# Memory attention with a spatial gate on one core: the memories' products in two single PSUM banks instead of one tile of two banks

## The chip, the cores and the metric

The kernel runs on one core of one Trainium2 chip. What is measured is the time of the whole program on the device in microseconds, lower is better: a median of runs, and beside it one execution that the hardware profiler took, from which all rows below come.

## The reference, cut to what matters

Eight batches b, eight heads of width 64, 576 positions, 32 memories a head. An attention over memories is followed by a feed-forward layer with a spatial gate:

```
a = softmax(phi);  k_m = a^T k;  v_m = a^T v          # 32 memories a head
attn = softmax(scale * q k_m^T) v_m                   # 576 x 64 a head
x = attn, heads side by side                          # 576 x 512 a batch
h = relu(x @ w_in); u, v = halves of h                # 512 columns each
v_n = (v - mean(v)) / sqrt(var(v) + 1e-6)             # over the 512 columns
v_s = w_spatial @ v_n + b_spatial                     # over the 576 positions
out = (u * v_s) @ w_out
```

## The kernel before, in words

The attention's output is never formed. `products` multiplies the memories' values `vT` by `w_in` first; the result, "the memories' products" mp, is 256 memories (two halves r of 128 partitions) by 1024 columns (two halves f of 512: f = 0 for u, f = 1 for v). The attention weights then multiply it. Every full-precision product is made of three products of short parts: a value x is kept as a high part (mh, ah, vh, gh) and a low part (ml, al, vl, gl), and the terms high x high, high x low and low x high are summed in PSUM.

The work is cut into steps, each written as a Python generator that yields after every piece. The capital letter is the kind, the digit the tile:

- P: weights of the memories from phi (DMA, maxima on DVE, transposes mt and mb on PE, `cmb` on ACT, subtraction on DVE, exponential on ACT, sums `es` on POOL or DVE).
- K: `kvm` (144 small matmuls), the sums' reciprocal `den`, `kmn` and `vmn` on ACT, the transposes `tk` and `tv`, copies `kT` and `vT`.
- Q: q by DMA, four transposes `qT` on DVE. S: scores `sc` on PE into four banks (r, c), four transposes out of them on DVE (L547), the softmax on DVE and ACT (`rmx`, `sm`, `rsum`), transposes `aT`, then `ah` on ACT and `al` on DVE for either half.
- M0, M1: the products for f = 0 and 1: the matmuls mp (L603) for both halves r in turn, then, half by half, `mh` on ACT (L612) and `ml` on DVE (L153; for a few of the first two batches by PE and ACT). 
- V0 to V4: rows of v: `pv` on PE, relu on ACT, mean and variance on DVE (`bn`, L681), a few numbers on POOL (`few`), normalisation on ACT, `vh` on ACT and `vl` on DVE.
- U0 to U3: `pu` on PE in two halves, relu `u` on ACT. G0 to G3: the spatial product `ps` on PE in four pieces (the first three take `vh`, `vl` of V0, V1, V2; the last V3 and V4), then `g` on DVE (L769), `gh` on ACT, `gl` on DVE. O0 to O4: `po` on PE in two halves, copy `o` on ACT, DMA out.

Below, ps1.0 is the first piece of G1, pu0.1 the second half of U0, po3.0 the first half of O3.

Nothing reorders the steps. Three tables of letters, `START` (first batch, with the loading and decoding of the weights), `PLAN` (the body of the loop, batches 1 to 5) and `END` (the last two batches) say in which order the pieces are written, a mark ' meaning the next batch. Every engine works its own instructions in the written order, and SP's DMA queue too, so a waiting instruction holds up all that stands behind it on its engine. Z in `START` is a matmul on a constant whose result nobody reads (`warm_up`, tile `idle`); there are 25 of them.

PSUM has eight banks. Two pools share them: four tiles of one bank (`bank`) and two tiles of two banks (`banks`):

```
    ps1 = ctx.enter_context(tc.tile_pool(name="ps1", bufs=4, space=PSUM))
    ps2 = ctx.enter_context(tc.tile_pool(name="ps2", bufs=2, space=PSUM))
```

A new tile waits until the last reader of the tile that had its place is done. Before, mp, pu and ps share the two tiles of two banks; sc, kvm, pv, po and the small transposes share the four single banks.

Of the kernel before, what the change touches and what calls it, by code (L numbers as in the profile page):

```python
# [19 lines left out]
START = """  # L20
    P Z P*2 Z P*2 Q P*9 Q P Q P Q K Q*4 K Q*2 P Z Q Z Q Z D1 K W E0 K W K*2 Z D0 K*2 E0*2 Z K*4
    S Z S K S*2 W S T1 D1 Z L0 S*2 T1 D0 Z X0 T4 Z T3 Z T3 S T1 S X1 T1 S E1 Z E0 S*3 Z T4 Z T4
    T3 L0 Z S*2 L1 T3 E1 S Z T4 Z*2 T0 S E1 S T4 X1 Z E1 T0 S L0 L1 T0 S*2 Z M1*2 S*2 X1 L0 L1
    P' S M1 L1 P' X0 P' T2 Z X0*2 M1 B S M1 B Q' K' S P' M1 S T2 P' M0 S V0 M0*2 V0 T2 P' Z V4
    M0 P'*3 V2 V1 V0 Z T2 M0 V4 X1 U1 P' X0 P' V0*2 X0 V0 M0 V1 V0 P' V3 P' M0 U1 V2 V4 V1 X0 K'
    P' V4 U0 P' V2 U1 U0 K' Q' K' V4 U0 V1*2 V2 V1 U2*2 V2 Q' V1 U3 Z U3 U2 V3 V4 G1 V2 V3 U3
    P'' G1 Q' K' V4 V3 X1 V2 V4 G1 G2*2 Q' V3 G2 K' V3 V4*2 P'' V3 K'*2 P'' G2 X1 Q' K' P'' G2
    X1 X3 P'' K'' G2 K' X2 G2 K'' K' G1 P'' X3 P'' X3 P'' G1 X3 G0 G1 G0 G1 K' G1*2 G0 P''*2 G0
    X2 G3 G2 K' P'' G3 X2 G2 S' M1' X2 G0 X2 P'' G3 G0*2 S'*2 O0 P'' X2 X3 G3 X2 X3 S' O2 X3 S'
    M1'*2 S' G3 G0 O3 G3 G0 G3 S' M1' O3 O1 S'*2 O3 P'' O1 P'' S' Q'' O1 S' G3 M1' S' G3 O0 S'  # L30
    O3 O2 S' M1' S' O0 S'*5 O2 K'' O0 K'' Q'' O2 O1 K''*2
"""

PLAN = """
    M0 V0 V4 V1 V0 U1 U3 V2 V0 U3 U0 K' U0 V1*2 Q' P'' V2 V3 P'' V4 V0 V1 P'' U2*2 V3 S' V2*2 U0
    M0' M1' V3 S' S S' P'' U2 P''*2 V2 K'' M0'*2 V3 M0'*2 M1'*2 K'' G1 M1' V3 G1 V2 V4 P'' M1'
    P'' K''' S' G0*2 V3 V2 V4*2 G1 V3 P''' G0 S' G0 S' G1 G3 K'' S' G0 G3 S' G3 G0 G2*2 G1 K''*3
    M1' K'' G1 S' G0 G1 P''' G0 S'*2 G1 G3 O1 S' G2 G1 S' M0 S' P''' G3 S'*2 G3 G0 G3 G2 O0 G3*2
    S'*2 G2 Q'' O2 G2 S' V1' G2 O1 V0' O3 V1' O1 V1' P''' O1 G2 O0 O1 V0' M1 O0 G2 K'' U3' Q''
    S' O3 V0' V4' O2 P''' Q'' O4 K'' Q'' O3 V4' O0 O4 V4' U1'*2 P''' O2 V4' O4 O2 O4 O0 V4' P'''  # L40
    K'' Q'' K''' O3
"""

END = """
    V0 V1 V4 V1 V0 V1 K' U3*2 V0 V2 V0 U2 V2 U1 U2 V1 V3 V2*2 U2 V2 V3 U0*2 M0' U0 M1' Q' S' V4
    M0' V3 G1 M0'*2 M1' G1 V3 M0' M1'*2 V3 G0 M1' V2 V4 S' V2 V3 G0 G1 V4 S' G0 S'*2 V3 V4 S' G0
    S' G0 S' G1 G3 G0 G1 G0 S' G3 G1 G3 S' G3 S'*2 U1 G2 S' G2 G0 G1 G0 V4 G2*2 S'*3 G1 O3 S' G1
    G3 U1' S'*2 V0' V2' S' V1' G2 V0' U1' V1' U1' V0' O0 U0' O2 U0' U3' V2' G2 V3' U0' G3 V4 G2
    V1' V2' V0'*2 G3 O2 G2 V0' U2' V2' U2' V0' O0 V2' U3' U2' G3*2 V1' G0' V4' V1' V3' O3 V2'
    V1' V3' V1' V4' O0 G0' V3' V4' U3' G1' V3' V4' V2' V3' V4' O1 Q' G0' G2 G1' V3' V4'*2 O1 V4'  # L50
    Q' G1' O3 V4'*2 G1'*3 G0' G2' G1' G2'*2 G1' G0' G2' G0' G3' G0'*2 O1 G3' G0' G3'*2 O2 O0 O1'
    G3' O1 G3' G1' G2'*2 O4' O3' G2' O2 O0' G2' G3' O1'*3 O0' O3' G3' V4 O3' O3 O3' G2' G3' K'
    O0' O4' O0' O2' O4' O2'*2 O4' O2'
"""
# [837 lines left out]
```

## Time and profile before

| what | value |
|---|---|
| median of 3 runs | 436.64 us (435.97 to 437.99) |
| the profiled execution | 436.06 us, of which the span of instructions is 434.3 us |
| PE (TensorE matmuls) busy | 405.9 us, 93% of the span |
| DVE / ACT / POOL busy | 275.1 / 230.6 / 102.5 us |
| PE in the first 50 us | 38.3 us busy |
| mean granted TensorE clock | 0.979 of full |
| bytes moved | 50.68 MB, mean 117 GB/s |

PE is the engine that is nearly always at work, so what another engine does matters where PE stands still for it. The profile draws a matmul longer than the step to the next one (a pair of 288 columns is drawn 0.42 us long and the next pair begins after 0.26 us), so idle time that it prints for PE is a little less than what was lost.

### The profile page before, as it was taken

To read this page: it belongs to the slowest core of one execution; us is meant where nothing else is said; L and a number is where in the kernel's file an instruction comes from. 1 tells how busy PE (TensorE), PEld (TensorE's weight loads), DVE (VectorE), ACT (ScalarE), POOL (GpSimd) and SP (SyncE) were. 2 spreads that over 40 slices of the span, in tenths; PEclk is the share of its full clock that TensorE was granted. 3 is DMA by queue.
4 is the path that set the end of the run, shared out by engine and by line. 5 is a ranking of instruction groups with operands and counts; after the bars stand their busy time and mean duration, and the time that the engine had idled before them with its cause. 6 is when DMAs were issued, how large, how long until landed. Compare 5 with 4: busy or idle time off the path is not lost.

```text
span 434.3 us, 9318 instructions
## 1 busy us (share of the span) xinstructions
PE 405.9 (93%) x3882; PEld 344.1 (79%) x3882; DVE 275.1 (63%) x492; ACT 230.6 (53%) x444; POOL 102.5 (24%) x191
## 2 busy tenths in 40 slices
PE   3799999998989999999899999999899998999996
PEld 2675689786789887988698887988698877888985
DVE  3269548886889257974589357964697347934420
ACT  2538797446754377345753376335853374337412
POOL 1376473203200114012501014022401110023100
...
GB/s 305 365 381 249 74 76 207 146 27 250 150 208 12 105 163 129 110 26 154 83 219 2 103 183 160 60 54 142 121 2 2 127 51 2 0 2 24 2 48 145
DMA packets 85725, 50.68 MB, mean 117 GB/s; under 512 B 66162, under 2 KB 70258, under 8 KB 85684
## 3 DMA queue, kind: packets, MB, share of 16 engines
...
q14 instruction: 11, 0.09, 0.1%
...
## 4 chain that ended last, share of the span: by engine, by line
PE 47%; DVE 20%; ACT 14%; DMA 8%; POOL 5%; issue 4%; SPq 1%; POOLq 0%; DVEq 0%; ACTq 0%
PE po L798 18%; PE ps L758 14%; PE pv L636 6%; PE pu L720 4%; ACT vr L693 4%; DMA raw<-in_moe_w_in_dram 3%; DVE ml L153 3%; DVE vl L698 3%; DVE rmx L553 2%; DVE sm L556 2%; ACT mh L612 2%; DMA out_dram<-o 2%; ACT vh L696 2%; DVE phi_sb L311 2%; DMA q_sb<-in_q_dram 1%
## 5 line engine op out<-in xcount | busy, mean ns | idle before, releaser
L758 PE MATMUL ps<-wth,vh 128*128 128x288 f32 x256 | 57.3, 305 | 7.4 <-DVE ml L153 4.1
L758 PE MATMUL ps<-wtl,vh 128*128 128x288 f32 x256 | 54.6, 294 | 0.0
L758 PE MATMUL ps<-wth,vl 128*128 128x288 f32 x256 | 54.5, 294 | 0.0
L758 PEld LDWEIGHTS ps<-wth,vh 128*128 128x128 f32 x256 | 40.8, 188 | 13.1 <-issue 4.4
L798 PE MATMUL po<-woh,gh 128*128 128x512 f32 x128 | 50.4, 394 | 0.2 <-DVE sm L547 0.2
L798 PE MATMUL po<-wol,gh 128*128 128x512 f32 x128 | 50.3, 393 | 0.0
L798 PE MATMUL po<-woh,gl 128*128 128x512 f32 x128 | 50.2, 392 | 0.0
L804 ACT COPY o<-po 128x512 f32<-128x512 f32 x36 | 21.1, 585 | 46.1 <-PE po L798 35.1
L758 PEld LDWEIGHTS ps<-wtl,vh 128*128 128x128 f32 x256 | 41.4, 188 | 0.0
L758 PEld LDWEIGHTS ps<-wth,vl 128*128 128x128 f32 x256 | 40.9, 188 | 0.0
L681 DVE BATCH_NORM_STATS2 st<-vr 128x6 f32<-128x512 f32 (+1 forms) x35 | 24.0, 684 | 22.9 <-ACT vr L678 22.8
L684 POOL TENSOR_SCALAR few<-few 128x1 f32<-128x1 f32 (+1 forms) x35 | 9.7, 276 | 120.1 <-DVE few L682 105.3
L693 ACT ACTIVATE vr<-vr,few 128x512 f32<-128x512 f32 (+1 forms) x40 | 32.5, 815 | 8.9 <-POOL few L688 8.9
L586 POOL CAST ar<-ah 128x128 fp32r<-128x128 f32 x7 | 6.1, 874 | 130.2 <-ACT ah L579 130.2
L433 DVE STREAM_TRANSPOSE qT<-q_sb 128x576 f32<-128x576 f32 x28 | 20.2, 753 | 23.6 <-DMA q_sb<-in_q_dram 19.0
L698 DVE TENSOR_TENSOR vl<-vr,vh 128x512 fp32r<-128x512 f32 x32 | 22.0, 691 | 20.5 <-ACT vh L696 19.6
L720 PE MATMUL pu<-ah,mh 128*128 128x288 f32 x128 | 28.9, 307 | 0.1
L579 ACT CAST ah<-aT 128x576 fp32r<-128x576 f32 x14 | 9.4, 675 | 36.3 <-DVE aT L575 36.3
L798 PEld LDWEIGHTS po<-woh,gl 128*128 128x128 f32 x128 | 24.1, 188 | 5.5
L153 DVE TENSOR_TENSOR ml<-mp,mh 128x512 fp32r<-128x512 f32 x28 | 18.8, 688 | 15.1 <-ACT mh L612 15.1
L798 PEld LDWEIGHTS po<-woh,gh 128*128 128x128 f32 x128 | 24.1, 188 | 5.1 <-issue 0.4
L720 PE MATMUL pu<-ah,ml 128*128 128x288 f32 x128 | 27.4, 296 | 0.4 <-ACT ml L151 0.4
...
## 6 DMA issues: line engine op xcount, KB each, us to landing
...
```

Source lines behind the costliest of these rows:

```text
L153: nc.vector.tensor_tensor(lo, x, hi.bitcast(F32), op=ALU.subtract)
L433: nc.vector.transpose(qT[:, 2 * n : 2 * n + 2].rearrange("p h s -> p (h s)"), q_sb[:, 2 * n : 2 * n + 2].rearrange("p h i d -> p (h i d)"),)
L579: nc.scalar.copy(ah[:, r], aT[:, r])
L636: nc.tensor.matmul(pv, x[:, r, cs], m[:, r, DM:DFF], start=(n == 0), stop=(n == 5))
L681: nc.vector.bn_stats(st6, vr)
L684: nc.gpsimd.tensor_scalar_add(rs, mv[:, 1:2], 1e-6)
L693: nc.scalar.activation(vr, vr, AF.Identity, bias=sh, scale=rs)
L698: nc.vector.tensor_tensor(vl[:, st, :], vr, vh[:, st, :].bitcast(F32), op=ALU.subtract)
L720: nc.tensor.matmul(pu[:, hf, 0:HALF], m[:, r, cs], a[:, r, hf * HALF : (hf + 1) * HALF], start=(n == 0), stop=(n == 5),)
L758: nc.tensor.matmul(ps[:, hf, 0:HALF], a, w[:, hf * HALF : (hf + 1) * HALF], start=(n == 0), stop=(n == len(ops) - 1),)
L798: nc.tensor.matmul(po, a, w, start=(n == 0), stop=(n == 11))
L804: nc.scalar.copy(o, po)
```

## The change

`products` takes two tiles of one bank each instead of one tile of two banks. So mp leaves the pool `ps2` to pu and ps, and takes two of the four places of `ps1`. The three tables are written anew.

```diff
         cs = slice(f * 512, (f + 1) * 512)
-        both = banks(f"mp_{b}_{f}")
-        mps = [both[:, r] for r in range(2)]
+        mps = [bank(f"mp_{b}_{f}_{r}") for r in range(2)]
         for j in range(NJ):
             for r in range(2):
                 nc.tensor.matmul(
...
 PLAN = """
-    M0 V0 V4 V1 V0 U1 U3 V2 V0 U3 U0 K' U0 V1*2 Q' P'' V2 V3 P'' V4 V0 V1 P'' U2*2 V3 S' V2*2 U0
...
+    M0 K' S Q' V0 V4 V1 V3 U1 V4 V0*2 V2 U3 U2 P'' U2 K'' V3 P'' U2 V0 V2 P''*2 U0 V2 V4 V2 G1
...
```

The same matmuls, copies and transfers are written for every batch as before. Of the matmuls on the constant (Z), 14 are left of 25. In the built program mp of f = 0 takes the two banks that held the scores of r = 0, `kvm` the two that held those of r = 1, and mp of f = 1 the two banks of f = 0 again. The half r = 1 of `mh` waits only for PE; before, it waited for DVE as well.

The first place is PE where batch 3's scores, products and then `kvm` of batch 4 stand. Names are tile_indices_number; sc_1_1 is the bank of r = 1, c = 1. Before:

```order
L536 MATMUL sc_1_0_2020<-qT,kT 32x288
L536 MATMUL sc_1_1_2021<-qT,kT 32x288
L603 MATMUL mp_0_2047<-win_sb,vT 32x512 x8
L603 MATMUL mp_1_2056<-win_sb,vT 32x512 x8
L338 MATMUL kvm_0_2078<-kv_sb,phi_sb 32x128
L338 MATMUL kvm_1_2079<-kv_sb,phi_sb 32x128
```

After, for the same batch (the last two rows are the first two of eight such):

```order
L536 MATMUL sc_1_0_2019<-qT,kT 32x288
L536 MATMUL sc_1_1_2020<-qT,kT 32x288
L757 MATMUL ps_1_2010<-wth,vh 128x288 x2
L757 MATMUL ps_1_2010<-wtl,vh 128x288 x2
L757 MATMUL ps_1_2010<-wth,vl 128x288 x2
L719 MATMUL pu_0_1992<-ah,mh 128x288 x2
L719 MATMUL pu_0_1992<-al,mh 128x288 x2
L719 MATMUL pu_0_1992<-ah,ml 128x288 x2
L602 MATMUL mp_0_0_2065<-win_sb,vT 32x512
L602 MATMUL mp_0_1_2066<-win_sb,vT 32x512
```

The products of f = 0 now stand behind a piece of ps and a half of pu; `kvm` of the next batch follows them, then three pieces of ps0, and only then the products of f = 1 (mp_1).

The second place is DVE behind the last `bn` of batch 2: the transposes out of the scores (sm<-sc), the low parts of the products (ml) and what stands around them. Before:

```order
L547 STREAM_TRANSPOSE sm<-sc_0_0_2018 128x288
L547 STREAM_TRANSPOSE sm<-sc_0_1_2019 128x288
L153 TENSOR_TENSOR ml<-mp_0_2047,mh 128x512 x2
L153 TENSOR_TENSOR ml<-mp_1_2056,mh 128x512 x2
L547 STREAM_TRANSPOSE sm<-sc_1_0_2020 128x288
L698 TENSOR_TENSOR vl<-vr,vh 128x512
L706 TENSOR_TENSOR t_1794<-vr,t_1794 64x512
L698 TENSOR_TENSOR vl<-vr,vh 128x512
L547 STREAM_TRANSPOSE sm<-sc_1_1_2021 128x288
L553 TENSOR_REDUCE rmx<-sm 128x36
L556 TENSOR_TENSOR sm<-sm,rmx 128x1152
```

After:

```order
L547 STREAM_TRANSPOSE sm<-sc_0_0_2017 128x288
L547 STREAM_TRANSPOSE sm<-sc_0_1_2018 128x288
L547 STREAM_TRANSPOSE sm<-sc_1_0_2019 128x288
L547 STREAM_TRANSPOSE sm<-sc_1_1_2020 128x288
L553 TENSOR_REDUCE rmx<-sm 128x36
L697 TENSOR_TENSOR vl<-vr,vh 128x512
L153 TENSOR_TENSOR ml<-mp_0_0_2065,mh 128x512
L556 TENSOR_TENSOR sm<-sm,rmx 128x1152
L153 TENSOR_TENSOR ml<-mp_0_1_2066,mh 128x512
L705 TENSOR_TENSOR t_1756<-vr,t_1756 64x512
L697 TENSOR_TENSOR vl<-vr,vh 128x512
L561 TENSOR_REDUCE rsum<-sm 128x36
```

All four transposes come first now, ml of f = 0 is split by the softmax's steps, and ml of f = 1 stands further down, behind two transposes aT.

The third place is ACT around the high parts mh of the same batch. Before:

```order
L729 ACTIVATE u<-pu_2_2003 128x576
L693 ACTIVATE vr<-vr,few 128x512
L612 CAST mh<-mp_0_2047 128x512 x2
L612 CAST mh<-mp_1_2056 128x512 x2
L693 ACTIVATE vr<-vr,few 128x512
L696 CAST vh<-vr 128x512
L702 CAST t_1794<-vr 64x512
L696 CAST vh<-vr 128x512
L704 CAST t_90<-vr 64x512
```

After:

```order
L728 ACTIVATE u<-pu_0_1992 128x576
L695 CAST vh<-vr 128x512
L611 CAST mh<-mp_0_0_2065 128x512
L703 CAST t_90<-vr 64x512
L692 ACTIVATE vr<-vr,few 128x512
L695 CAST vh<-vr 128x512
L611 CAST mh<-mp_0_1_2066 128x512
L558 ACTIVATE sm<-sm 128x1152
L779 CAST gh<-g 128x512
L611 CAST mh<-mp_1_0_2189 128x512
L579 CAST ah<-aT 128x576
L611 CAST mh<-mp_1_1_2190 128x512
```

The four copies mh stood in one block; now each stands alone, those of f = 1 behind the softmax's exponential (L558) and the first gh.

## Rows read from the trace of the kernel before

**Rows 1.** The page: the span, and the busy time of each engine.

```profile
span 434.3 us, 9318 instructions
PE 405.9 (93%) x3882; PEld 344.1 (79%) x3882; DVE 275.1 (63%) x492; ACT 230.6 (53%) x444; POOL 102.5 (24%) x191
```

**Rows 2.** Busy time by engine in four stretches, each from the start of a batch's scores to the start of the next batch's (batches 2 to 5). Columns: stretch, its length, then busy time and number of instructions of PE, weight loads, DVE, ACT and POOL, granted TensorE clock, DMA share, GB/s.

```profile
114.61:163.85 49.24, 48.11 (x464) 41.39 (x463) 34.19 (x65) 26.07 (x51) 7.07 (x17) 1.00 0.45 112
163.85:211.03 47.18, 45.24 (x452) 39.36 (x451) 32.62 (x61) 24.71 (x48) 10.21 (x21) 1.00 0.52 111
211.03:260.10 49.07, 47.95 (x465) 41.47 (x464) 32.86 (x61) 26.12 (x51) 9.63 (x21) 1.00 0.51 113
260.10:307.31 47.21, 45.23 (x452) 39.34 (x451) 32.59 (x61) 24.58 (x48) 10.22 (x21) 1.00 0.57 117
```

**Rows 3.** PE in order of time behind the scores of batch 3: start, length, what; in brackets the idle time before it and what ended it.

```profile
163.85 1.20 PE L536 MATMUL sc<-qT,kT 64*32 64x288 f32 x32
164.85 1.92 PE L603 MATMUL mp<-win_sb,vT 64*32 64x512 f32 x32
166.56 2.22 PE L338 MATMUL kvm<-kv_sb,phi_sb 64*32 64x128 f32 x144
169.55 0.50 PE L758 MATMUL ps<-wth,vh 128*128 128x288 f32 x2 [0.76 <-DVE ml L153]
170.94 0.43 PE L758 MATMUL ps<-wth,vl 128*128 128x288 f32 x2
171.49 0.50 PE L758 MATMUL ps<-wth,vh 128*128 128x288 f32 x2
...
177.90 0.54 PE L758 MATMUL ps<-wth,vh 128*128 128x288 f32 x2 [0.36 <-DVE g L769]
```

**Rows 4.** ACT, then DVE, in order of time in the same stretch.

```profile
166.77 0.57 ACT L612 CAST mh<-mp 128x512 fp32r<-128x512 f32 x1
168.09 1.07 ACT L612 CAST mh<-mp 128x512 fp32r<-128x512 f32 x2 [0.76 <-DVE ml L153]
170.03 0.59 ACT L612 CAST mh<-mp 128x512 fp32r<-128x512 f32 x1 [0.87 <-DVE ml L153]
...
167.37 0.69 DVE L153 TENSOR_TENSOR ml<-mp,mh 128x512 fp32r<-128x512 f32 x1 [1.15 <-ACT mh L612]
168.71 1.29 DVE L153 TENSOR_TENSOR ml<-mp,mh 128x512 fp32r<-128x512 f32 x2 [0.65 <-ACT mh L612]
170.65 0.69 DVE L153 TENSOR_TENSOR ml<-mp,mh 128x512 fp32r<-128x512 f32 x1 [0.65 <-ACT mh L612]
```

**Rows 5.** PE in order of time, five other places where it stood still: before a transpose mb, in the last two batches (two), in the first batches (two).

```profile
209.18 0.33 PE L305 MATMUL mb<-ident,cmb 128*128 128x128 f32 x1 [0.71 <-ACT cmb L302]
...
361.34 0.51 PE L758 MATMUL ps<-wth,vh 128*128 128x288 f32 x2 [1.27 <-DVE ml L153]
...
370.26 0.53 PE L758 MATMUL ps<-wth,vh 128*128 128x288 f32 x2 [0.93 <-DVE g L769]
...
80.08 1.09 PE L603 MATMUL mp<-win_sb,vT 64*32 64x512 f32 x16 [0.59 <-DVE g L769]
...
102.85 0.50 PE L636 MATMUL pv<-mh,ah 128*128 128x512 f32 x1 [1.08 <-ACT vr L678]
```

**Rows 6.** What DVE does from the end of batch 2 to the end of batch 3's softmax: five rows of DVE in order of time, the first matmul of pv that needs it, the busy time of the stretch between (columns as in rows 2), and two groups of the page (busy time, mean ns of one, idle before).

```profile
162.38 1.36 DVE L311 TENSOR_TENSOR phi_sb<-phi_sb,mb 128x1152 f32<-128x1152 f32 x1 [1.39 <-PE mb L305]
163.65 0.69 DVE L681 BATCH_NORM_STATS2 st<-vr 128x6 f32<-128x512 f32 x1
165.41 0.81 DVE L547 STREAM_TRANSPOSE sm<-sc 128x288 f32<-128x288 f32 x2
173.92 0.48 DVE L547 STREAM_TRANSPOSE sm<-sc 128x288 f32<-128x288 f32 x1
189.45 0.76 DVE L581 TENSOR_TENSOR al<-aT,ah 128x576 fp32r<-128x576 f32 x1
...
189.81 0.39 PE L636 MATMUL pv<-mh,ah 128*128 128x512 f32 x1
...
165.41:190.21 24.80, 23.57 (x310) 21.47 (x295) 21.22 (x39) 12.01 (x25) 5.11 (x10) 1.00 0.47 96
...
L769 DVE TENSOR_TENSOR g<-u,ps 128x576 f32<-128x576 f32 x32 | 23.2, 742 | 5.7 <-PE ps L758 5.5
L782 DVE TENSOR_TENSOR gl<-g,gh 128x512 fp32r<-128x512 f32 x32 | 22.2, 708 | 8.3 <-ACT gh L780 8.2
```

**Rows 7.** The granted clock in the first 58 us: two stretches at half (columns as in rows 2), and the products of batch 0, f = 1 and then f = 0.

```profile
20.40:34.00 13.60, 11.51 (x156) 8.68 (x149) 9.50 (x16) 5.18 (x7) 9.76 (x5) 0.50 1.04 343
44.30:47.60 3.30, 3.30 (x20) 1.26 (x21) 2.67 (x4) 1.71 (x4) 2.17 (x3) 0.50 1.61 138
...
39.13 1.09 PE L603 MATMUL mp<-win_sb,vT 64*32 64x512 f32 x16
44.60 1.96 PE L603 MATMUL mp<-win_sb,vT 64*32 64x512 f32 x16
```

**Rows 8.** Prices for what the change adds: PE where it goes from kvm to ps without a wait, and the scaling on ACT between the sums of kvm and the transpose tk.

```profile
312.94 0.44 PE L338 MATMUL kvm<-kv_sb,phi_sb 64*32 64x128 f32 x11 [0.66 <-issue]
313.31 0.54 PE L758 MATMUL ps<-wth,vh 128*128 128x288 f32 x2
...
179.58 0.62 ACT L357 ACTIVATE kmn<-kvm,den 128x128 f32<-128x128 f32 x2 [0.69 <-DVE den L353]
```

More of the change, by code (lines that the diff above doesn't have):

```diff
@@ L20 @@
 START = """
[L21 to L31, printed above, removed]
+    Z P*10 Q P K P Z K D1 Q*2 P Q P D0 P*2 Q Z P Z Q*4 E0 Z Q K W Q K E0 K Q W Z K*2 Z K E0 K Z
@@ new lines @@
+    K E0 K Z D1 Z K S L0 S T1 L0 K S T1 D0 S*2 W T3 T1 Z S*5 T4 T3 E1 S*2 T3 T1 T3 L1 E1 L0 S E1
+    S*4 L0 T4 T2 X0 T4 E1 S L1 X0 B S*3 P' T4 Z X1 Z*2 P' T4 T2 X0 X1*2 S*2 Q' P' L1 P' S*2 P'
+    M1 S X0 M1 L1 M1 X0 K' M1 T2*2 T0*2 M1 B M0 S M1 P' S T0 M0 P' V0 X0 V0 X1 M0 X0 M0 V1 V2 U1
+    M0 Q'*2 V0 V1 M0 P' V2 V1 Q' M0 P' V2 V3 P' V0 V1 U0 K' V0 U0 V0 U1 P' V4 K' U2 Q' V0 U3 X1
+    V1 U0 V4 V2 K' P'*2 U1 V4 P' U2 V1 P' V2 U3 V4 P'' Q' X2 V3 V2 K' V1 V4 K' U2 V2 G2 V3 U3 V4
+    P'' V3 K' V4 K'' K' V4 X3 G2 V3 G2 P''*2 K' P'' G1 Q'' G1 V3 K' V4 K' P'' G1 V4 V3 G1 P'' G1
@@ L32 @@
+    X1 P'' X2*2 K' G2 K' X1 G2 P'' G1*2 G0 G2 G1 P'' G0 X2 G2 X3 P'' G1 G0 G3 X2 G0*2 G2 S' X3
+    G2 G3 X3 G3 G0 G3 S' G0 X3 S' P'' S' M1' X2 X3 M1' O3 S'*2 M1' G3 O0 X2 G3 M1' X3 Q'' G3 S'
+    P'' S' P''*2 S' G3 O0 K'' O2 O3 S' O0 M1' S' O2 G0 O3*2 S'*2 M1' O1 O0 S' G3 O1 S' O2 O1
+    S'*3 G0 O1 O2
 """
 PLAN = """
-    M0 V0 V4 V1 V0 U1 U3 V2 V0 U3 U0 K' U0 V1*2 Q' P'' V2 V3 P'' V4 V0 V1 P'' U2*2 V3 S' V2*2 U0
-    M0' M1' V3 S' S S' P'' U2 P''*2 V2 K'' M0'*2 V3 M0'*2 M1'*2 K'' G1 M1' V3 G1 V2 V4 P'' M1'
@@ L37 @@
[L37 to L41, printed above, removed]
+    M0 K' S Q' V0 V4 V1 V3 U1 V4 V0*2 V2 U3 U2 P'' U2 K'' V3 P'' U2 V0 V2 P''*2 U0 V2 V4 V2 G1
@@ new lines @@
+    S' P'' G1 M1 V3 P'' V2 V4 V3 U0 S' M0' U0 S' V2 P'' M0' S'*3 V2 K'' V4 M0' G0 P'' V3 S' V3
+    P'' M0' G0*2 M0' V4 K'' S' M1' K''' V3 K'' G0 G1 S' G0 G1 S' G0 S' G1 G0 K'' S' G2 M1' S'*2
+    M1' S' M1' P''' K'' G2*2 G3 G1*2 G3*3 G1 M1' S' P''' K'' G0*2 S' G3 S'*2 O3 K'' G1 G3 G2 S'
+    V1' Q'' G3 V0' G2 M0 V1' O1 V4' G3 G2 V0' G2 V4' O1 V1' O0*2 U3' G2 P''' V4' V1' Q''*2 P'''
+    V1' O4 O0 O1*2 G3 O2 O0 M1 O2 K'' O3 O2 O0 P''' O3 Q'' K'' U1' K'' G2 U3' Q''' O3 O4 V1' O2
+    P''' O1 O4 V0' V4' O4 U1'
@@ L42 @@
 """
 END = """
[L45 to L53, printed above, removed]
+    V0 Q' K' U1 V2 V0 V2 V3 V0 V1 V4 V2 U2*2 U0 V4*2 V2 U0 M0' U3 U2 V3 V0 V4*2 U0 V2 V3 M1' M0'
+    G1 V3 M0' G0 M0' M1' G0 G1 M1' M0' V2 M1' V3 S' M1' V2 V3*2 V4 S' G0 S'*2 G1 G0 G1 S'*2 G3
@@ new lines @@
+    G0 S' G3 G1 G2 S'*2 G2 G1*2 G0 G1 G0 S' G0 G2 S' G2 S' G1 S' G2 U1 S' G3 O3 G0 S' O2 S'*2
+    G2*2 S' G3 S' U1' G3 V1' S' V2' G3 V0' V1' G3 V0' O3 V1' V0' G3 U0' V1' V0' O2 V2' V4' O2 O3
+    U0' V0' G2 V2' V0' V4' V0' U0' V1' V2' U1'*2 G2 V4' O1 V3' U3' V4' U3' V4' V1' K' O3 O0 V2'
+    U2' V4'*2 U2' V1' V3'*2 O0 U2' O1 O2 G1' U3' V4' V2' U3 V3' G0'*2 V4'*2 O0 G3 V2' V3'*2 G0'
+    V4 G1'*2 V3' G0' G1' G0' G1' G2'*2 G1'*2 G0' G2' G1' G0' G1' G2'*2 O2' G2' G3' G2' G3'*2 O1
+    G0' G3' O3' G2' G0' G3' V1 G3' G2' V1 G3' O0 O0' G3' O4' O0'*3 G3' O4' O2' O4' O1 Q' O4'
@@ L54 @@
+    O3'*2 O1'*2 O3' O2' V1 O2' Q' O1' V4 O1'
 """
```

## The prediction

> **What bounds the kernel now.** I read the page first: PE works 405.9 of 434.3 us, 93%, and no other engine comes near [rows 1]. A change that leaves PE's work alone can only win back the time in which PE stands still. Then the stretches from one batch's scores to the next: of 47 to 49 us PE is idle 1.13, 1.94, 1.12 and 1.98 us [rows 2]. So the loop has little left. Then the time line of PE at a hand-over, that is behind the scores of the next batch, where nearly all of that idle time lies. There ps waits 0.76 us for the last reader of mp's tile; a second ps begins 0.55 us after the pair before it where 0.26 is usual, so 0.28 more is lost without being printed; and a third waits 0.36 us for g, which with the 0.17 that the drawn end hides (0.43 less 0.26) is 0.53 [rows 3]. The time line of ACT and DVE says why the first two happen: mh and ml of the four halves go strictly in turn. ACT stands 0.76 and 0.87 us for ml before it copies the other half, although PE had finished that half long ago, and DVE stands 0.65 us for each mh [rows 4]. The chain lasts from 166.77 to 171.34, 4.6 us, and two tiles of two banks are held until it ends.
>
> Here a rule of the Trainium skill and the rows part. The page "PSUM — Partial Sum Buffer", section "Specifications (TRN2)", lets ScalarE and VectorE work in PSUM side by side at full bandwidth as long as they don't meet in one bank. The two halves were in different banks before too, so by the page alone nothing would be gained by parting the tile; ACT's 0.76 and 0.87 us show that the program's own wait on the tile kept them apart. I go by the rows.
>
> **The change part by part.** What goes:
>
> 1. The wait of ps for ml: ps no longer shares places with mp. At four hand-overs (scores at 114.61, 163.85, 211.03, 260.10) 0.76 + 0.28 = 1.04 us each, 4.2 us; I count nothing for the fifth, at 307.31, whose row at that place is a wait on "issue" [rows 8]. In the last two batches 1.27 [rows 5], and 0.28 more by the estimate that the next ps steps there as in the loop [rows 3]: 1.55. Together 5.7.
> 2. The wait of ps for g, 0.53 at each of five hand-overs, is late work of DVE behind ml; with ml spread out, g follows its ps in time (below): 2.65. In END 0.93 + 0.17 = 1.1 goes, but there the four ml still stand ahead of the softmax, and going through DVE's new order I find 0.8 back at ps3 and ps2: 0.3. Together 2.95.
> 3. The wait of PE for mb, 0.71 + 0.17 = 0.88 [rows 5], at every second batch, two times: 1.75. In the new order the copy cmb stands ahead of u2 and relu2, before PE reaches mb.
> 4. In the first batches mp of batch 1 waits 0.59 for g, and pv 1.08 + 0.17 for a relu that frees its bank [rows 5]. Now mp stands behind three pieces of ps3, and the four pv have four banks: 1.85.
>
> Gone: 12.25 us.
>
> What comes:
>
> 5. Switches. kvm stands between pu and ps, the scores between two ps. From kvm to ps without a wait takes 313.31 - 312.94 = 0.37 us, of which 11 small matmuls at 2.22/144 us are 0.17: 0.20 a switch [rows 3, 8]. Two to three more per hand-over, 0.5 us, six hand-overs: 3.0.
> 6. For batch 2, tk and tv stand right behind the sums of kvm. PE then waits for den and kmn: kmn begins 0.69 us after ACT is free and lasts 0.62 [rows 8]; with vmn behind it I take 1.5. Its cover was a whole batch; once only.
> 7. ps1.0 now stands 0.8 us behind pu2.1, whose u must free its place: some 0.1 at five hand-overs, 0.5.
> 8. The start. PE's clock is at half from 20.4 to 34.0 and from 44.3 to 47.6 us, with the matmuls on the constant running between [rows 7]; 11 of these go. Three of the old ones stood in dense work, about 0.23 each (a pv matmul's step), 0.7 saved. The dense work starts in both orders when the last low parts of the first batch are through, and neither order of DVE is clearly ahead. Bounds for the clock: the old second stretch cost 1.96 - 1.09 = 0.9 in mp [rows 7] and at most half of the remaining 1.4 us, so 1.6 could be won; a stretch as long as the first in dense work would cost 6.8. The row nearest in time is the short one, so I take 0.7 lost, against the 0.7 saved: 0.
> 9. w_in's pieces are loaded in another order and q of the next batch is issued earlier. In START the bytes ahead of the last piece are the same; in the loop the earlier q takes a wait from DVE, none from PE. Nothing.
>
> Coming: 5.0. The balance is 7.25 us.
>
> Whether DVE lets PE have it is the question, so I went along DVE at a hand-over (S is the start of the scores). phisub (1.27 to its successor) and two bn (1.76, from 163.65 to 165.41) stand ahead of the transposes [rows 6]. mb is done at S - 1.4, so the first transpose starts at S + 1.6, the second ends at S + 2.5, the fourth at S + 3.3. PE has scores 1.0, a switch, ps1.1 and pu0.1 at 0.79 each: mp wants its banks at S + 2.8, kvm at S + 3.65. Both fit, by 0.3. ml of f = 0 is done near S + 7.9, mp of f = 1 wants those banks at S + 8.7. Fits. The softmax: from the first transpose to the end of al DVE worked 21.5 of 24.8 us [rows 6]. Of this the new order puts one g (0.74), two gl or parts of them and two maxima behind al, 1.9 us; and the waits for mh, 1.15 and twice 0.65 [rows 4], go, while some 2 us of waits for ps and for gh remain. al then ends at 1.6 + 19.6 + 2.0 = S + 23.2. In the trace al ended 26.4 us after the scores' start. PE reaches the matmul of pv1 that reads it at S + 23.3 (21.2 of work, 0.9 of switches, five matmuls of pv). That is no slack at all, so I set 0.2 us a hand-over aside, 1.0.
>
> 436.06 - 7.25 + 1.0 = 429.8 for the execution that was profiled; the median is 0.58 above that execution, so 430.4, and I say 430.
>
> **The rivals.**
>
> A. DVE becomes the bound. For: the walk above ends 0.1 us apart, and the stretch was 87% busy. Against: of its 3.3 us idle (24.80 less 21.47 [rows 6]) 2.45 was waiting for the turn of mh and ml [rows 4], which goes. If al is 1 us late at five hand-overs, 5 of the 7.25 go back: 434.
>
> B. The clock. Fewer matmuls on the constant leave PE less busy between 20 and 44 us, and a low stretch of 13.6 us [rows 7] reaching over dense work costs 6.8 where 1.6 is paid now: 5 more, 435. Against: from 36 us on the new order gives PE nearly unbroken work even at half. The Trainium skill's page "TensorE: Matmul & The Clock Gate", Part 1, has the gate set by how busy PE has lately been, which speaks against taking such matmuls out; the trace doesn't decide it: in the low stretch from 20.4 us PE was drawn busy for 11.51 of 13.60 us [rows 7].
>
> C. Slower: the banks of the scores. Before, mp and kvm did not wait for the fourth transpose, which came 10.1 us after the scores' start (173.92 less 163.85 [rows 3, 6]); now mp needs the banks of the first two and kvm those of the others, at once. What pays for it is the 0.3 us above. It decides from 1.5 us of delay in the chain u2, relu2, bn2, transposes (7.25/6 + 0.3). At 2 us late, (2 - 0.3) x 6 = 10.2 are lost against 7.25 won: 439.6.
>
> D. Nothing moves: the waits are only renamed, for instance ps waits for u and g instead of ml for 0.9 us a hand-over. 435 to 437.
>
> **How the numbers follow.** My forecast, 427 to 433, gets 0.62. A gets 0.16, B 0.06, D 0.09, C 0.07. The low end: the balance with only one switch a hand-over (1.8 us less) and the best clock (1.6) gives 430.4 - 1.8 - 1.6 = 427, and without the reserve 426; with the first batch some 1.5 us earlier, 424.5. The high end takes in A and B: 435.5. By 0.5% (2.2 us, about what a measurement of this kernel tells from no change) faster means below 434.4: the forecast, most of A and a part of B, 0.80. Same: D and the rest, 0.13. Slower: 0.07.
>
> **What would show it.** After the change ACT's mh should have no idle time that ml ended, and PE's ps none that ml ended (point 1); PE idle in a batch's stretch should fall from 1.1 to 2.0 us to below 0.7 (points 1 to 3). If pv waits on al, or on ah, by 0.3 us or more in each batch, it is A; if mp or kvm waits on the transposes (L547), it is C; if ps waits on u or g for more than 0.5 us a batch, D. The granted clock between 44 and 55 us decides B. I'd be wrong altogether if PE's busy time itself rose by more than the 3 us of switches.

## The result and the profile after

The changed kernel takes 425.5 us (median of 4 runs, 425.06 to 426.42) where the kernel before took 436.9 (435.97 to 437.99): ratio 0.974, 95% interval 0.971 to 0.977. Measured once more on another chip the ratio was 0.9743 (0.9709 to 0.9776). It is faster by 11.4 us; the forecast was 6.6. The 427 to 433 us that got the chance of 0.62 do not hold the result; the outer ends of the range, 424.5 and 435.5, do. The profiled execution took 425.26 us, 10.8 less than the one of before. The page's head:

```profile
span 423.5 us, 9286 instructions
PE 403.7 (95%) x3871; PEld 340.3 (80%) x3871; DVE 272.7 (64%) x492; ACT 226.7 (54%) x444; POOL 103.5 (24%) x191
```

PE is busy 2.2 us less than in [rows 1], but only because 11 matmuls on the constant are gone: the 25 were drawn busy for 12.15 us, the 14 that are left for 7.38. Without them PE's busy time rose by 2.5 us. Of the 10.8 us, 8.6 are idle time. The four stretches from one batch's scores to the next, which answer to [rows 2] with the same columns:

```profile
112.56:161.05 48.49, 48.49 (x465) 41.56 (x464) 33.68 (x65) 25.11 (x50) 7.13 (x17) 1.00 0.51 126
161.05:206.52 45.47, 45.47 (x452) 39.24 (x451) 32.42 (x61) 24.53 (x49) 11.15 (x21) 1.00 0.44 116
206.52:254.79 48.27, 48.27 (x464) 41.46 (x463) 32.43 (x61) 25.02 (x50) 11.47 (x21) 1.00 0.44 114
254.79:300.27 45.48, 45.48 (x452) 39.24 (x451) 32.43 (x61) 24.54 (x49) 11.15 (x21) 1.00 0.47 119
```

Length and PE's busy time are the same number: in the loop no idle time of PE is left that the profile can see. The hand-over behind batch 3's scores, PE in order of time, answers to [rows 3]:

```profile
161.05 1.20 PE L536 MATMUL sc<-qT,kT 64*32 64x288 f32 x32
162.18 0.54 PE L757 MATMUL ps<-wth,vh 128*128 128x288 f32 x2
...
163.08 0.43 PE L719 MATMUL pu<-ah,mh 128*128 128x288 f32 x2
...
163.97 1.09 PE L602 MATMUL mp<-win_sb,vT 64*32 64x512 f32 x16
164.85 1.38 PE L338 MATMUL kvm<-kv_sb,phi_sb 64*32 64x128 f32 x80
166.16 0.53 PE L757 MATMUL ps<-wth,vh 128*128 128x288 f32 x2
...
168.75 1.16 PE L338 MATMUL kvm<-kv_sb,phi_sb 64*32 64x128 f32 x64
169.65 1.12 PE L602 MATMUL mp<-win_sb,vT 64*32 64x512 f32 x16
```

No row has a bracket. ACT and DVE there, as in [rows 4], and at the end of the softmax the first matmul of pv that reads al of r = 1:

```profile
165.41 0.58 ACT L611 CAST mh<-mp 128x512 fp32r<-128x512 f32 x1
167.79 0.58 ACT L611 CAST mh<-mp 128x512 fp32r<-128x512 f32 x1
...
162.48 1.54 DVE L547 STREAM_TRANSPOSE sm<-sc 128x288 f32<-128x288 f32 x4
166.15 0.68 DVE L153 TENSOR_TENSOR ml<-mp,mh 128x512 fp32r<-128x512 f32 x1
168.40 0.69 DVE L153 TENSOR_TENSOR ml<-mp,mh 128x512 fp32r<-128x512 f32 x1 [0.30 <-ACT mh L611]
183.00 0.76 DVE L581 TENSOR_TENSOR al<-aT,ah 128x576 fp32r<-128x576 f32 x1
...
184.46 0.39 PE L635 MATMUL pv<-mh,al 128*128 128x512 f32 x1
```

The four transposes end at 164.02, 3.0 us behind the scores' start. The first two, done by half of their 1.54 us (163.25), free mp's banks 0.7 us before PE comes to them, and kvm, which needs the banks of the other two, has 0.8 to spare. al ends at 183.76, 0.7 before the matmul that needs it. These are the margins on which the new order lives.

What idle time ended the copies mh in the whole program, after and then before (columns: us, times):

```profile
L611 ACT CAST mh<-mp x32: 572/580/599, 42.3 to 352.0; 128x512 fp32r<-128x512 f32 x32
  PE mp L602: 2.4, 3
```

```profile
L612 ACT CAST mh<-mp x32: 564/586/595, 40.3 to 361.8; 128x512 fp32r<-128x512 f32 x32
  DVE ml L153: 10.8, 14
```

The 10.8 us of turns between ACT and DVE are gone. What PE still waits for, from the list of PE's waits (us in total, times, longest); all but two of them lie in the first 45 us:

```profile
PE mt L296 <- DVE mx L283: 4.4, 2, 3.5
PE wt L246 <- issue: 3.3, 1, 3.3
...
PE tk L370 <- ACT kmn L357: 0.9, 1, 0.9
PE at L506 <- DVE sm L499: 0.8, 2, 0.5
```

The two are tk at 97.3 us (0.94) and one of the two mt, at 109.7 (0.83).

**Where the 10.8 us come from.** To lay the traces side by side although matmuls changed places, I counted for each moment the work PE had done by then (every useful matmul at the usual step of its kind, those on the constant left out) and compared the two times at which the same amount was done. Lead of the changed kernel:

| stretch of the kernel before | lead at its end | won in it | the prediction's sum |
|---|---|---|---|
| first batch, to 62 us | 2.5 | 2.5 | 0 |
| rest of START, batch 2's hand-over (114.61), to 162 us | 2.9 | 0.4 | 0.35 + 0.77 |
| four hand-overs (163.85, 211.03, 260.10, 307.31), to 349 us | 7.9 | 5.0 | 3.8 |
| last two batches | 10.9 | 3.0 | 1.35 |

Behind the last matmul 0.1 us goes back. In the last column a hand-over is 1.04 + 0.53 us that go, less 0.5 + 0.1 that come and 0.2 of reserve, with 0.88 more where mb stands.

### The profile page after: what moved, and what is told of

Read it like the earlier page. It is cut to its first block, busy times and chain, and to the rows that moved or that the text cites. A ratio compares the mean times of both kernels' runs of the same rounds, so it can differ in the third digit from the quotient of the medians.

```text
span 423.5 us, 9286 instructions
## 1 busy us (share of the span) xinstructions
PE 403.7 (95%) x3871; PEld 340.3 (80%) x3871; DVE 272.7 (64%) x492; ACT 226.7 (54%) x444; POOL 103.5 (24%) x191
## 4 chain that ended last, share of the span: by engine, by line
PE 71%; DVE 9%; ACT 8%; DMA 7%; issue 2%; SPq 1%; POOL 1%; ACTq 0%; DVEq 0%
PE ps L757 23%; PE po L797 19%; PE pu L719 9%; PE pv L635 8%; DMA w_sb<-in_moe_w_spatial_dram 4%; PE mp L602 3%; PE kvm L338 3%; PE sc L536 1%; DMA raw_out<-in_moe_w_out_dram 1%; DMA out_dram<-o 1%; DMA phi_sb<-in_phi_dram 1%; ACT vr L692 1%; DVE ml L153 1%; DVE sm L547 1%; ACT vr L664 1%
## 5 line engine op out<-in xcount | busy, mean ns | idle before, releaser
L680 DVE BATCH_NORM_STATS2 st<-vr 128x6 f32<-128x512 f32 (+1 forms) x35 | 23.8, 681 | 42.2 <-ACT vr L677 42.0
L757 PEld LDWEIGHTS ps<-wth,vh 128*128 128x128 f32 x256 | 41.4, 189 | 6.6 <-issue 3.3
L779 ACT CAST gh<-g 128x512 fp32r<-128x512 f32 x32 | 19.6, 619 | 35.6 <-DVE g L768 35.6
L768 DVE TENSOR_TENSOR g<-u,ps 128x576 f32<-128x576 f32 x32 | 23.8, 743 | 12.5 <-PE ps L757 12.5
L781 DVE TENSOR_TENSOR gl<-g,gh 128x512 fp32r<-128x512 f32 x32 | 22.2, 698 | 9.9 <-ACT gh L779 9.8
L797 PEld LDWEIGHTS po<-wol,gh 128*128 128x128 f32 x128 | 24.1, 188 | 4.9
```

The lines of the kernel that those rows point to most:

```text
L680: nc.vector.bn_stats(st6, vr)
L757: nc.tensor.matmul(ps[:, hf, 0:HALF], a, w[:, hf * HALF : (hf + 1) * HALF], start=(n == 0), stop=(n == len(ops) - 1),)
L768: nc.vector.tensor_tensor(g.rearrange("p (a s) -> p a s", a=2), u[:, dt, :].rearrange("p (a s) -> p a s", a=2), ps[:, :, 0:HALF], op=ALU.mult,
L779: nc.scalar.copy(hi, x)
L797: nc.tensor.matmul(po, a, w, start=(n == 0), stop=(n == 11))
```

## The experiments

**Are the turns the cause, or the banks?** In the kernel before, with its tile of two banks and its three tables, only the order in which a tile is read changes, from batch 2 on (the first two batches keep the old order):

```diff
         for r in range(2):
             nc.scalar.copy(mh[:, r, cs], mps[r])
             yield
-            yield from low(f"ml{b}{f}{r}" if b < 2 else None, ml[:, r, cs], mps[r], mh[:, r, cs])
+        for r in range(2):
+            yield from low(None, ml[:, r, cs], mps[r], mh[:, r, cs])
```

> The kernel before, its tile of two banks and its tables kept; from batch 2 on, only the four steps that read one tile mp are written in another order: both high parts mh first and then both low parts ml, where it was mh, ml, mh, ml. My theory: what cost time was that readers of one tile take turns, ACT and DVE alternately. With one turn a tile instead of three, ACT can go on with the second tile while DVE works on the first. From the trace before: ml of the first tile would end at 169.1 instead of 169.4 and that of the second at 170.4 instead of 171.3, so ps wins 0.25 and 0.28 us and g some 0.5: 1.0 us at each of five to six hand-overs, 430 to 432 us. Rival: DVE's own four ml are what takes the time, in whichever order: 435.5 to 437 us.

Measured: 430.5 us (428.3 to 432.8), ratio 0.986 (0.983 to 0.990). Half of the whole gain, with the tile as it was. ACT, DVE and PE at the hand-over of batch 3:

```profile
165.86 2.03 ACT L618 CAST mh<-mp 128x512 fp32r<-128x512 f32 x4
...
166.94 2.48 DVE L153 TENSOR_TENSOR ml<-mp,mh 128x512 fp32r<-128x512 f32 x4 [1.63 <-ACT mh L618]
...
168.38 0.51 PE L765 MATMUL ps<-wth,vh 128*128 128x288 f32 x2 [0.49 <-DVE ml L153]
```

The four mh run without a break and the four ml too; the chain lasts 3.6 us (165.86 to 169.42) where it lasted 4.6. The first ps still waits 0.49 of 0.76 us, the second ps and the ps behind g no longer wait. So the turns were the cause, and what is left of the wait, 0.49 us, is the time of DVE's own ml. The four loop stretches are 48.19, 46.01, 47.94 and 46.36 us here. The first and the third are shorter than the changed kernel's 48.49 and 48.27; in the other two PE still waits for mb (0.67 and 1.01 us), which the new tables removed. So at the hand-over itself reading in blocks, on the old tile, gives as much as the parted tile with its new order. No run has the new tables on the old tile, so the rest of the gain, in the first and the last batches above all, is not divided between tile and tables. The Trainium skill's rule on banks ("PSUM — Partial Sum Buffer", section "Specifications (TRN2)"), against which the prediction weighed its rows, is not contradicted: the banks are the same in both orders, and only the program's waits differ.

**The tile alone.** The kernel before with two single tiles and its own order, except that in the loop two transposes move up (without that mp of f = 1 would wait for ever):

```diff
-    ... V3 S' S S' P'' U2 ... P'' K''' S' G0*2 V3 V2 V4*2 G1 V3 P''' G0 S' G0 S' G1 ...
+    ... V3 S' S S'*3 P'' U2 ... P'' K''' G0*2 V3 V2 V4*2 G1 V3 P''' G0*2 S' G1 ...
-        both = banks(f"mp_{b}_{f}")
-        mps = [both[:, r] for r in range(2)]
+        mps = [bank(f"mp_{b}_{f}_{r}") for r in range(2)]
```

> The kernel before with two single tiles for mp and nothing of the new order, except that in the loop the third and fourth transpose out of the scores stand right behind the first two (otherwise mp of f = 1 could never get its banks). My theory: the parted tile by itself is no gain, since mp and kvm now wait for banks. From the trace before, with S the start of the scores: transposes done at S + 2.5 (first two) and S + 3.3, so mp starts at S + 2.5 instead of S + 1.0, and kvm, which takes the banks of mp f = 0, at S + 5.3 instead of S + 2.7; ps no longer waits for ml (1.0 us back). Net 1.5 to 2 us lost at each of five hand-overs, and 1.0 in the last two batches: 446 us (442 to 450). Rival: parting the tile is what pays, and the order is a detail: the 0.76 + 0.28 us at each hand-over go and little comes, 431 to 433 us.

Measured: 449.5 us, ratio 1.028 (1.023 to 1.034). PE behind the scores of batch 3:

```profile
173.79 1.20 PE L535 MATMUL sc<-qT,kT 64*32 64x288 f32 x32
175.84 2.31 PE L601 MATMUL mp<-win_sb,vT 64*32 64x512 f32 x32 [0.85 <-DVE sm L546]
178.73 0.40 PE L337 MATMUL kvm<-kv_sb,phi_sb 64*32 64x128 f32 x2 [0.58 <-DVE ml L152]
```

mp starts 2.05 us behind the scores' start and kvm 4.9 (expected 2.5 and 5.3). Each loop stretch is 0.7 to 1.2 us longer than in [rows 2] (50.38, 48.18, 50.30, 47.87). Most of the rest, 8.8 us, is lost in the first batches, up to batch 2's scores at 123.41 instead of 114.61, which I had not counted: there too mp waits for transposes (1.9 us at 85.1), and pv 1.4 us for ml (at 109.3). The granted clock was also at half from 55.9 to 59.3 and from 86.6 to 90.0 us, where the kernel before had full clock; how the 8.8 us divide is open. The parted tile without the order is a loss, in the loop by some 1.0 us a batch.

**The filling.** The changed kernel with mp of f = 0 straight behind the scores, in the loop:

```diff
-    ... V2 G1 S' P'' G1 M1 V3 P'' V2 V4 V3 U0 S' M0' U0 S' ...
+    ... V2 G1 S' M0' P'' G1 M1 V3 P'' V2 V4 V3 U0 S' U0 S' ...
```

> The changed kernel with the products of f = 0 put straight behind the scores in the loop, ahead of the piece of ps and the half of pu that fill the time there. My theory (banks of the scores): mp then waits for the second transpose, which ends 2.2 us after the scores' start while PE gets there after 1.0: 1.2 us of idle time on PE before mp, released by the transpose, at five hand-overs, 6 us, so 430.5 to 432 us (ratio to before 0.985 to 0.989). Rival: the transposes are not what holds mp, or PE makes the time up later in the batch: 425 to 426.5 us.

Measured: 432.1 us (431.9 to 433.4), ratio 0.991 (0.988 to 0.994).

```profile
163.75 1.20 PE L536 MATMUL sc<-qT,kT 64*32 64x288 f32 x32
165.69 1.45 PE L602 MATMUL mp<-win_sb,vT 64*32 64x512 f32 x16 [0.74 <-DVE sm L547]
```

mp starts 1.94 us behind the scores' start instead of 1.0, and a stretch of the loop is 1.35 us longer than after (46.84 and 49.62 against 45.47 and 48.27). So the piece of ps and the half of pu between scores and mp are what rival C was held off with.

**DVE's slack.** The changed kernel with one reduction done twice:

```diff
         nc.vector.tensor_reduce(rmx, smf, axis=AX.X, op=ALU.max)
+        nc.vector.tensor_reduce(rmx, smf, axis=AX.X, op=ALU.max)
```

> The changed kernel with the softmax's maximum taken twice (DVE does the 1.35 us reduction a second time in each batch from batch 1 on; the values stay the same). My theory: DVE is close behind PE, with some 0.5 to 0.7 us to spare (al of r = 1 ends at 183.76, the matmul of pv that reads it starts at 184.46; mp of f = 1 starts 0.6 us after the ml that frees its banks). So 0.65 to 0.8 us is lost in each of five to six batches: 429 to 430.5 us. Rival 1, DVE is already the bound: all of 1.35 us in each batch, 433 to 434 us. Rival 2, DVE's time doesn't matter here: 425.5 us.

Measured: 430.2 us (429.9 to 430.6), ratio 0.986 (0.982 to 0.990). The total is the expected one, but not its places: from batch 3 to batch 6 a stretch grows by 0.26 us only (45.75 and 48.53 against 45.47 and 48.27), so DVE has 1.1 us to spare there, more than I had read off. The loss sits at batch 2's hand-over, where mp of f = 1 waits for ml (1.4 us more in that stretch), and in the last two batches, where ps waits for g (1.3 drawn):

```profile
123.62 0.66 PE L603 MATMUL mp<-win_sb,vT 64*32 64x512 f32 x7 [0.46 <-DVE ml L153]
...
363.77 0.54 PE L758 MATMUL ps<-wth,vh 128*128 128x288 f32 x2 [1.30 <-DVE g L769]
```

The last 0.8 us were lost before 76 us, where this kernel is the changed one; there its low stretch of the clock ended 0.6 us later (below).

**First batch and last batches by themselves.** The changed kernel with one table of before: END, with a few letters shifted because the two loops leave off at different places, and START as it was (first lines of the two tables).

```diff
 END = """
-    V0 Q' K' U1 V2 V0 V2 V3 V0 V1 V4 V2 U2*2 U0 V4*2 V2 U0 M0' U3 U2 V3 V0 V4*2 U0 V2 V3 M1' M0'
+    V4 V0 V4 V0 K' U3 V0 V2 V0 U2 V2 U1 U2 V1 V3 V2*2 U2 V2 V3 U0*2 M0' U0 M1' Q' S' V4 M0' V3 G1
...
 START = """
-    Z P*10 Q P K P Z K D1 Q*2 P Q P D0 P*2 Q Z P Z Q*4 E0 Z Q K W Q K E0 K Q W Z K*2 Z K E0 K Z
+    P Z P*2 Z P*2 Q P*9 Q P Q P Q K Q*4 K Q*2 P Z Q Z Q Z D1 K W E0 K W K*2 Z D0 K*2 E0*2 Z K*4
```

> The changed kernel with the table of before for the last two batches. If the last two batches gained what the two traces show when they are laid side by side at equal work of PE, 3.0 us: 428.5 us (ratio 0.981). If they gained what the prediction's sum had for them (1.55 + 0.3 less a hand-over's switches and reserve, 1.15 us): 426.7 us.

> The changed kernel with the table of before for the first batch (its 25 matmuls on the constant with it). If the first batch gained what the traces show at equal work of PE (2.2 us by 60 us into the run): 427.5 to 428.5 us. If it gained what the prediction's sum had for it (1.85 - 1.5 + 0, that is 0.35 us): 425.9 us.

Measured: END of before 428.0 us (0.9805, 0.976 to 0.985), 2.5 above the changed kernel and 2.9 longer in span. START of before 437.5 us (1.003, 1.000 to 1.005), far above both expectations. Neither is the old table at its old price: with single tiles both meet waits that they did not have. In END the scores wait for banks that mp holds; in START a matmul on the constant waits 2.2 us for its bank and mp of batch 1 for the transposes:

```profile
352.30 2.51 PE L535 MATMUL sc<-qT,kT 64*32 64x288 f32 x32 [1.35 <-DVE ml L152]
...
56.38 0.51 PE L816 MATMUL idle<-minus 128*128 128x512 f32 x1 [2.19 <-ACT vr L664]
...
83.81 1.04 PE L602 MATMUL mp<-win_sb,vT 64*32 64x512 f32 x9 [1.75 <-DVE sm L547]
```

The two waits shown for START are 3.9 us of the 11.8 by which batch 2's scores come later (124.33 against 112.56); tk (1.5) and pu (1.2) wait there too, and the granted clock is at half from 119.9 to 123.3 us. What the two runs show is that each table belongs to its set of tiles. They don't price the first batch, and the last two only roughly.

**The matmuls on the constant.** The kernel before without the last 11 Z of its START (the first two of them in the first diff), and the changed kernel with 11 Z more behind the first scores:

```diff
-    ... S*3 Z T4 Z T4 T3 L0 Z S*2 L1 ...
+    ... S*3 Z T4*2 T3 L0 S*2 L1 ...
```

```diff
-    ... D1 Z K S L0 S T1 L0 ...
+    ... D1 Z K S Z*11 L0 S T1 L0 ...
```

> The kernel before without the last 11 of its matmuls on the constant. If these only take their own steps on PE, three of them in dense work: 436.2 us, 0.7 less than before. If the clock hangs on them (rival B): the stretch at half clock before 47.6 us gets longer, 438 to 440 us. If DVE sets the time there, as it is busy nearly without a break from 34 to 47 us: no difference, 436.6 to 437.

> The changed kernel with 11 more matmuls on the constant, all behind the first scores, where PE stands idle for a load from 22.7 to 27.5 us. If the half clock from 24.7 to 41.3 us in the changed kernel comes from PE standing still there and costs time, it starts later or goes, and the run gets 1 to 2 us shorter: 424 us. If DVE sets the time up to 43 us: 425.5 us, whatever the clock does. If the filling delays the transposes of w_spatial: 426 to 427 us.

Measured: without 11 of them the kernel before takes 436.8 us, ratio 1.002 (1.000 to 1.004): their 0.7 us are not won, and of the three expected outcomes it is the last by its time. The granted clock of its profiled execution (stretches at half, columns as in [rows 2]):

```profile
22.60:32.90 10.30, 8.08 (x57) 5.77 (x55) 7.56 (x13) 4.75 (x7) 8.19 (x3) 0.50 1.08 371
43.10:49.90 6.80, 6.46 (x26) 3.47 (x27) 3.80 (x6) 3.32 (x7) 2.62 (x3) 0.50 1.09 100
```

The second stretch reaches to 49.9 us, into dense work, instead of to 47.6 [rows 7]; just ahead of it, from 40.6 to 43.0 us, PE stood still for 2.43 us, waiting for mh. But the run that reads mp in blocks, which keeps all 25, has its second low stretch from 42.8 to 49.6 us, so the missing ones are not shown to be the reason, and the end of a low stretch varies (below). What the median says is that the 0.7 us don't come; why is open. With 11 more the changed kernel takes 428.6 us, ratio 0.983 (0.979 to 0.986), 3 us slower. The trace shows the third reason expected, at more than its size: a Z takes one of the four single banks, so it waits for DVE to read the scores, and w_spatial's transposes wt stand behind the Z, the first at 31.1 us instead of 23.8:

```profile
25.43 0.47 PE L815 MATMUL idle<-minus 128*128 128x512 f32 x1 [0.66 <-DVE sm L481]
28.00 3.31 PE L815 MATMUL idle<-minus 128*128 128x512 f32 x9 [2.11 <-issue]
31.10 1.06 PE L245 MATMUL wt<-ident,w_sb 128*128 128x128 f32 x4
```

Its last low stretch of the clock also lasts to 46.4 us, where the changed kernel's ended at 41.5; the run does not part the two.

**The two waits that are left.** Three versions of the changed kernel, each with another end of START: kvm of batch 2 ahead of the last half of po; pv of st = 0 between kvm and tk with mx ahead of a vl; and that with one u ahead of a normalisation.

```diff
-    ... S' G3 O1 S' O2 O1 S'*3 G0 O1 O2
+    ... S' G3 K''*3 O1 S' O2 O1 S'*3 G0 O1 O2 K''*4
```

```diff
-    S'*3 G0 O1 O2
+    S'*3 G0 O1 O2 M0'*5 K''*4 S'*2 K''*3 V0' K''*4 Q''*4 V0'*3 V4'*5 V1'*6 P'''*5
```

```diff
-    ... V4'*5 V1'*6 P'''*5
+    ... V4'*5 V1'*4 V3' U1'*3 P'''*5 V1'*2
```

> The changed kernel with the sums kvm of batch 2 put ahead of the last half of po of batch 0 instead of behind mp of batch 1. The po then covers den and kmn, so the waits of PE for kmn (0.94 and what follows, 1.3 us in all) and, since phi of batch 3 can be loaded earlier, for mx (0.83 drawn, 1.0) go: 423.2 to 424.5 us. Rival: kvm at the earlier place waits for its banks or for v of batch 2, and nothing is won: 425.5 us.

> The changed kernel, with the start of batch 1 in the loop written out in another order once: pv of st = 0 between the sums kvm of batch 2 and the transposes tk and tv, so that it covers den, kmn and vmn; and DVE's four steps mx of batch 3 ahead of a vl that waits for ACT. If these two are what PE waits for at 97.3 and 109.7 us: 1.3 us and 1.0 us go, and the run takes 423.2 us, 0.55% less than the changed kernel beside it. Rival: the steps moved ahead make pv or u late, as with the sums put earlier: no gain, or 0.5 us lost.

> The kernel of the run before last (pv of st = 0 between the sums and the transposes of batch 2, the steps mx of batch 3 earlier) with one more step moved in the same batch: the relu u of dt = 1 ahead of the normalisation of st = 1 on ACT, which stood 2.95 us waiting for POOL while that u, and behind it PE's pu, waited. If the gain of that run was only hidden by this wait (1.5 us lost before pu, as against 2.4 us won): PE's wait for u there goes, and the run is 0.3 to 0.5% below the changed kernel, ratio 0.970 to 0.972. If ACT is simply full there, the wait moves on to vh, cmb or the next u, and the ratio is that of the changed kernel, 0.973 to 0.975.

Measured: 428.4 us (0.982, 0.978 to 0.985), 425.0 (0.9732, 0.970 to 0.976) and 424.7 (0.9742, 0.972 to 0.977); the changed kernel beside the second took 425.0 (0.9743). None is distinguishable from the changed kernel but the first, which is slower. PE's waits in the three:

```profile
91.87 2.23 PE L337 MATMUL kvm<-kv_sb,phi_sb 64*32 64x128 f32 x142 [0.48 <-DVE ml L152]
99.34 0.50 PE L634 MATMUL pv<-mh,ah 128*128 128x512 f32 x1 [0.89 <-ACT kT L378]
```

```profile
108.14 0.53 PE L719 MATMUL pu<-ah,mh 128*128 128x288 f32 x2 [1.35 <-ACT u L728]
110.72 0.33 PE L305 MATMUL mb<-ident,cmb 128*128 128x128 f32 x1 [0.61 <-ACT cmb L302]
```

```profile
109.03 0.33 PE L305 MATMUL mb<-ident,cmb 128*128 128x128 f32 x1 [1.69 <-ACT cmb L302]
```

In the first, kvm waits for the bank of a low part and pv for the copy kT. The wait for mx, which was to go, is still there (0.83), pu waits 1.07 for u, and the granted clock is at half from 112.4 to 115.8 us, behind 2.4 us in which PE worked for 1.1. From batch 1's scores to batch 2's it takes 41.31 us, where the changed kernel took 37.50 and, executed again, 36.98.

In the other two the waits for kmn and mx are gone, but PE then waits for u and cmb, or for cmb alone. The same stretch lasts 36.21 and 35.69 us there, and from batch 2's scores on both take the changed kernel's 310.9 us. The 36.21 say little: that stretch began 1.3 us late, behind a low clock that ended at 44.0 us, and the run with mp straight behind the scores, whose order is the changed kernel's up to there, had 36.41 after a start that was 2.0 us late. The last one's profiled execution is 1.7 us shorter than the changed kernel's (span 421.8). The medians show no gain, and their intervals, 0.3% to either side, are too wide to rule out one of 1 us. The changed kernel stands.

> The changed kernel once more, on the same chip as the other two, as their measure: 425.5 us, ratio to before 0.974.

Measured: 425.0 us (424.8 to 426.4).

## Why the prediction was right in kind and short in size

Mechanism: right. By its own signs, mh has no idle time that ml ended, ps none that ml, u or g ended by more than 0.25 us, PE's idle time in a stretch fell from 1.1 to 2.0 us to zero (below the 0.7 asked), and PE's busy time without the matmuls on the constant rose by 2.5 us (below the 3 that would have been wrong altogether). Neither pv nor mp nor kvm waits for al or the transposes, so A, C and D did not come. C was a near miss by design: 0.7 and 0.8 us of margin, and moving the filling away costs 1.35 us a hand-over. A was priced on a walk that ended 0.1 us apart; the trace has 0.7 there, the double reduction shows 1.1, and of the 1.0 us of reserve nothing went to DVE. The walk had read the wrong column: 21.47 us of the 24.80 in [rows 6] are weight loads, DVE worked 21.22. With that it ends at S + 22.9, and in the trace al ends at S + 22.7 (183.76 less 161.05).

Point by point:

- Point 1, right for the four hand-overs it counted (0.64 to 0.76 drawn, all taken at 0.76). The step that failed is the fifth: "I count nothing for the fifth, at 307.31, whose row at that place is a wait on 'issue'". It was the same wait. DVE's rows of before at that place:

```profile
310.84 0.69 DVE L153 TENSOR_TENSOR ml<-mp,mh 128x512 fp32r<-128x512 f32 x1 [1.14 <-ACT mh L612]
312.19 1.29 DVE L153 TENSOR_TENSOR ml<-mp,mh 128x512 fp32r<-128x512 f32 x2 [0.65 <-ACT mh L612]
```

  The first of the two ml at 312.19 ends near 312.85, and PE goes on at 312.94 [rows 8]: the profile drew the stall 11 matmuls of kvm too early, and so found no semaphore for it. The kernel before without 11 Z has the same loop, and in its trace the wait stands at this place by its name:

```profile
315.02 0.72 PE L757 MATMUL ps<-wth,vh 128*128 128x288 f32 x2 [0.65 <-DVE ml L152]
```

  The four hand-overs gave 0.75, 1.75, 0.75 and 1.75 us, the last like the second; the sum had 0.77, 1.65, 0.77 and 0.61.
- Points 2 and 3, right: no wait for g in the loop, none for mb. In the last two batches 0.8 of the 1.1 us for g was thought to stay; ps loses there 0.25 at 361.04. Nor did the sum have what stood ahead of it, in rows that I had not looked at: mp waiting for u (0.38 drawn, 0.6 lost, at 358.01) and pu for u (0.3, at 351.8). Together these are 1.45 of the 1.65 us by which the last two batches gave more than 1.35.
- Point 4, right in what goes, short in what comes: beside kmn, mt waits 0.83 for mx at 109.7 us. The middle gave 0.4 instead of 1.1.
- Points 5 and 7, a little too cheap: two hand-overs of the loop, one of them with mb, gave 2.5 us (0.75 and 1.75), where 2 x 1.57 + 0.88 = 4.0 went; so 0.75 us a hand-over came, where the sum had 0.5 + 0.1. The reserve paid for it.
- Point 6, right: 0.94 drawn and 0.3 behind it, 1.3 us against 1.5.
- Point 8 is the largest miss: 0 where 2.5 us were won. PE's first pv starts at 45.91 us instead of 46.50, and by then PE has done a pair of wt's corrections on the constant and a transpose mt that the old kernel did at 48.76 and 49.02, 0.3 us: together 0.9. I had compared only DVE's orders and "what goes" of the Z, not which of PE's steps are done by the time the dense work starts. The rest of the second low stretch, which the changed kernel doesn't have, cost the old kernel 0.5 more (its first three pv took 1.32 us, 0.78 in the changed one), and two Z stood between there and 62 us, 0.5. A last 0.5 is a wait that no term had, in the kernel before:

```profile
56.88 0.54 PE L720 MATMUL pu<-ah,ml 128*128 128x288 f32 x2 [0.38 <-ACT ml L151]
```

  That makes 2.4 of the 2.5. These are counts from the two traces; no run separated the four, since the old START is no longer itself with single tiles.

That the outer range holds the result is in part luck. Its low end had the first batch 1.5 us earlier, which came and more, and one switch a hand-over, which did not come; the fifth wait and the waits in the last two batches, 2.8 us together, stood in none of its terms.

Rival B asked whether fewer Z let the clock stay low longer. In the profiled execution the one low stretch lasts from 24.5 to 41.5 us and ends before the dense work, so B did not come there. Where a low stretch ends is not fixed by the program:

```profile
24.50:41.50 17.00, 13.18 (x47) 8.13 (x54) 13.09 (x19) 11.98 (x19) 11.06 (x6) 0.50 0.97 282
```

```profile
36.70:40.10 3.40, 3.40 (x10) 2.31 (x11) 3.40 (x3) 2.89 (x5) 2.27 (x1) 0.50 0.91 321
```

```profile
24.50:45.00 20.50, 16.35 (x63) 9.71 (x62) 16.78 (x23) 13.76 (x22) 11.91 (x8) 0.50 0.99 273
```

These are the changed kernel, the same kernel again (the last of its two low stretches), and the one with mp straight behind the scores; all three have the same START. Batch 1's scores start at 75.06, 75.24 and 77.02 us. With the END of before (low until 41.4) it is 75.26, with the double reduction (42.2) 75.82, and in the second of the three last versions (44.0), whose START differs only behind this place, 76.35. So a low stretch that ends by 41.5 us goes with no delay, and one that ends 0.6, 2.5 or 3.4 us later with 0.8, 1.3 or 2.0: rival B is alive, but as a scatter of up to 2 us from one execution to the next. No run sets the clock by itself, so that the clock is the cause is not shown.

The Trainium skill's page "TensorE: Matmul & The Clock Gate", Part 1, says that the ramp at a kernel's start varies from run to run. These rows show a like scatter at the end of a later low stretch.
